# Hop propagation by one-hot matmuls: the order of the blocks in a hop, of the matmuls in a block and of the row fetches

## The chip, the cores and the metric

The kernel runs on one core of one Trainium2 chip. The metric is the device time of one execution in microseconds (us); before the change it is 4582.58 us, the median of three runs (4579.6 to 4584.72). The profile and its trace are of one further execution of 4621.35 us. Engines are named as in the profile: PE (TensorE; PEld are its weight loads), DVE (VectorE), ACT (ScalarE), POOL (GpSimd) and SP (SyncE, which only issues DMAs here).

## The reference

A graph has 10,000 nodes with 128 features and 160,000 edges. Seven times each node takes the weighted sum of the features of its edges' source nodes; the eight versions of every node (the input and seven hops) are then the tokens of a small attention block, which is not touched by the change.

```python
N, deg, D = 10000, 16, 128          # E = N * deg
h = x; toks = [x]
for _ in range(7):
    msg = h[src] * deg_inv_sqrt[src, None] * deg_inv_sqrt[dst, None]
    h = segment_sum(msg, dst, N)
    toks.append(h)
tok = stack(toks, axis=1)
# layernorm, self-attention over the 8 tokens, residual, readout -> (N, D)
```

## The kernel before, in words

**Blocks.** The nodes lie in `NT = 79` blocks of 128. A hop computes the new features of one block after the other from a table of all nodes' features, which is kept twice: in SBUF (`tab[i]`, a 16-bit value and a 16-bit rest, so 256 columns per node) and in HBM (`tabd[i]`). Hops alternate between two tables: hop `k` reads table `k % 2` and writes the other one.

**Edges of a block** are sorted by the block of their source. Sources in blocks 0 to 71 are read from SBUF by PE: `gather(jj)` (L469 to L479) multiplies one-hot 32-wide weight tiles with `tab[:, s, :]`, eight matmuls of 32 columns into one PSUM tile `p`; nine such groups make 72 matmuls. ACT or DVE copies each `p` to an SBUF tile `eb` (L478). `scat` (L441 to L448) then multiplies 128x128 one-hot weights with `eb` and sums into the PSUM tile `acc`: 18 matmuls per block. Sources in blocks 72 to 78 cannot be in that scheme; the block's edges from them (`og0`), and those few that found no free slot (`og1`, the overflow, from any node), are fetched row by row out of HBM by indirect DMAs that POOL issues (L434), and each takes one more 128-wide matmul into `acc`: `fetched` (L454) and the one with weights `Sov` (L464). So a block has 92 matmuls.

**Closing a block.** `over` (L458 to L467) does the `Sov` matmul, DVE sums the two halves of `acc` into `s` (L466), and `fin` (L591 to L598) writes the block's part of the next table: ACT (L593) and DVE (L594) into SBUF, DVE the block's largest value into `mx` (L596), a DMA on ACT's queue the rows to HBM (L597). `token_out` (L492) scales `s` into `r` on POOL (L494) and stores it from SP (L496).

**Order.** `pend` holds work that is put off: two groups of `scat` and the closing of block n-1 are done in block n, behind its gathers. So PE alternates between a gather phase and a scatter phase. The framework schedules the instructions of each engine at build time from the code's order; an engine then runs its own list strictly in order. A fetch waits for all DMA writes of the HBM table that it reads; `og` has two buffers for each of `og0` and `og1`, and SP loads the weights `w` of a block (592 KB, L602) up to four blocks ahead (five buffers).

**Hop 1** (L497 to L551) runs together with the making of the weights (`place`, `matrices`: DVE work above all), on the first table. **Between hop 1 and hop 2**, once the scale is known, ACT and DVE (L148, L149) make the new table in eight chunks, and SP writes each to HBM (L152). **Hops 2 to 7** (L576 to L606) start with a new scale from `mx`, the maximum over all blocks: a transpose on PE (L121), a reduction and four one-element steps on DVE (L123, L137 to L140), a matmul that spreads the value over the partitions (L129), and `c1` (L589), which `fin` needs. The last hop makes no new table and no scale.

**What the names are**: `tb`, `tbs`, `H`, `U`, `dsl` are small tiles of `place`, copied from PSUM by ACT (L329 to L365); `rb` is the row that `matrices` compares with the partition number, loaded by SP (L411); `gsd` are the weights in HBM.

Of the kernel before, what the change touches and what calls it, by code (L numbers as in the profile page):

```python
# [7 lines left out]
F32 = mybir.dt.float32  # L8
# [29 lines left out]
class Hops:  # L38
    def __init__(self, ctx, dp, missing, tc, x, src, dst, dis):
# [5 lines left out]
        self.tabd = [dp.tile([NT * 128, 256], F16, name=f"tabd{i}") for i in range(2)]  # L45
        self.tok = [None] + [dp.tile([NR, D], F32, name=f"tok{k}") for k in range(1, K + 1)]
# [70 lines left out]
    def colmax(self, pp, sp, col):  # L117

        nc = self.nc
        pm = pp.tile([128, 512], F32, name="pm", tag="acc")[0:1, 0:128]  # L120
        nc.tensor.transpose(pm, col, self.ident)  # L121
# [4 lines left out]
    def spread(self, pp, m, out):  # L126
        nc = self.nc
        pb = pp.tile([128, 512], F32, name="pb", tag="acc")[:, 0:1]
# [3 lines left out]
    def pow2(self, pp, sp, col, cap):  # L132

        V = self.nc.vector
        m = self.colmax(pp, sp, col)
# [6 lines left out]
        self.spread(pp, r, q[:, 0:1])  # L142
# [173 lines left out]
    def place(self, ts, got):  # L316
# [49 lines left out]
        V.tensor_scalar(self.oidx[:, a:b, :NI], msc[:, 16:16 + n * NI].rearrange("p (g i) -> p g i", i=NI), float(NG * 512 - 1), None, op0=ALU.add)  # L366
# [61 lines left out]
    def block(self, t, w, tab, tabd, pend, lag, runs, first, evac, fin, drain=True):  # L428

        nc, V, A, T, G = self.nc, self.nc.vector, self.nc.scalar, self.nc.tensor, self.nc.gpsimd  # L430
        og = []
        for i in range(NI + 1):
            o = self.ogp.tile([128, 256], F16, name=f"og{i}")
            G.indirect_dma_start(out=o, out_offset=None, in_=tabd,  # L434
                                 in_offset=bass.IndirectOffsetOnAxis(ap=self.oidx[:, t, i:i + 1], axis=0))
            og.append(o)
        m = 257 if first else 256
        acc = []


        def scat(e, jj):  # L441
            if not acc:
                acc.append(self.pacc.tile([128, 512], F32, name="acc", tag="acc"))
            for j in range(e.shape[1]):
                J = 2 * jj + j
                T.matmul(acc[0][:, :m], w[:, J * 128:(J + 1) * 128], e[:, j, :m], start=J == 0, stop=False)  # L446
                if J == 0 and t > 0:
                    fetched()  # L448


        def fetched():
            for i in range(NI):
                W = w[:, (NG + i) * 128:(NG + i + 1) * 128]
                T.matmul(acc[0][:, :256], W, og[i], start=False, stop=False)  # L454
                if first:
# [625 lines left out]
```

## Time and profile before

| what | value |
|---|---|
| median of 3 runs | 4582.58 us (4579.6 to 4584.72) |
| profiled execution | 4621.35 us |
| its span, first to last instruction | 4619.6 us |
| PE busy | 3902.3 us (84%), 69456 matmuls |
| DVE, ACT, POOL busy | 3437.1, 2441.3, 1853.7 us |
| granted PE clock, mean | 0.961 |
| DMA | 591.53 MB, 128 GB/s |

The profiled execution is 38.8 us (0.8%) longer than the median of the runs. In its span hop 1 lies from about 570 to 1343 us, hops 2 to 7 from there to 3865 us, at some 417 us each, and the attention from about 3870 us to the end. In the lines below a row of the timeline has its start in us from the span's start, its length in us, the engine, the line of the code and the tiles (out<-in); `[0.52 <-X]` is the idle time of that engine just before it and what ended it. An `x72` counts the instructions that are drawn together. Some matmul records are missing from a trace.

### The profile page before, as it was taken

What the parts mean: (1) busy time and instruction counts of PE and PEld (TensorE: products, weight loads), DVE (VectorE), ACT (ScalarE), POOL (GpSimd) and SP (SyncE); (2) the same over time, 40 slices, a digit from 0 to 9 for tenths busy, and PEclk for the clock granted to TensorE, in tenths of its full rate; (3) what the DMA queues carried; (4) which work ended last, traced back from release to release, by engine and by line L of the source; (5) the groups of instructions that cost most, each with busy time, mean ns of one, the idle gap of its engine ahead of it and who ended that gap; (6) DMA issues with size and microseconds to landing.
All of it is one profiled execution on the core that took longest, in us unless ns stands there. A gap on an engine that the chain in (4) does not pass through costs nothing. (4 is left out here: it accounts for less than half of the span.)

```text
span 4619.6 us, 162387 instructions
## 1 busy us (share of the span) xinstructions
PE 3902.3 (84%) x69456; PEld 3011.4 (65%) x69456; DVE 3437.1 (74%) x7291; ACT 2441.3 (53%) x5817; POOL 1853.7 (40%) x1977
## 2 busy tenths in 40 slices
PE   0566389999979999999999899999989997999996
PEld 0566366666656676767676667666767775777775
DVE  6888899999966666666666666666665555999998
ACT  3000045555565555555555555555555555777773
POOL 0000046656644454544444444444544443222221
PEclk9877689999989999999999999999999999999998
DMA  3000044444455555555555555555554554222220
GB/s 112 1 1 1 6 142 149 147 148 147 148 170 172 168 169 161 172 170 167 162 171 170 159 169 168 169 160 170 172 161 155 156 156 114 68 68 74 65 73 11
DMA packets 313745, 591.53 MB, mean 128 GB/s; under 512 B 55032, under 2 KB 206678, under 8 KB 307766
## 3 DMA queue, kind: packets, MB, share of 16 engines
q1 hardware_dynamic: 217925, 476.45, 32.8%
q0 software_dynamic: 35392, 72.55, 5.5%
q10 hardware_dynamic: 59696, 32.08, 2.5%
q8 instruction: 544, 8.91, 0.8%
q14 instruction: 188, 1.53, 0.1%
HBM read 455.43 MB, written 125.46 MB: 126 GB/s over the span
## 5 line engine op out<-in xcount | busy, mean ns | idle before, releaser
L478 ACT CAST eb<-p 128x512 f16<-128x512 f32 x3081 | 1637.7, 595 | 947.4 <-PE p L475 919.5
L434 POOL DMA_INDIRECT og<-tabd,oidx x1106 | 1219.7, 1103 | 2005.5 <-PE acc L454 1016.5
L478 DVE CAST eb<-p 128x512 f16<-128x512 f32 x1896 | 1181.6, 684 | 732.6 <-PE p L475 722.0
L475 PE MATMUL p<-tab,w 128*32 128x256 f16 x39816 | 1495.1, 275 | 208.7 <-DVE eb L478 92.9
L475 PEld LDWEIGHTS <-w 128*32 128x32 fp8e4 x39816 | 977.0, 96 | 645.6 <-issue 602.9
L446 PE MATMUL acc<-eb,w 128*128 128x256 f16 (+1 forms) x9954 | 1349.8, 275 | 9.5 <-DVE indeg L517 8.1
L446 PEld LDWEIGHTS <-w 128*128 128x128 fp8e4 x9954 | 916.3, 98 | 269.6 <-issue 165.0
L494 POOL TENSOR_SCALAR r<-s,ctok 128x128 f32<-128x128 f32 x553 | 452.8, 819 | 152.7 <-DVE indeg L517 67.4
L593 ACT ACTIVATE tab<-s,c 128x128 f16<-128x128 f32 x395 | 158.6, 401 | 296.2 <-DVE s L466 282.7
L594 DVE SCALAR_TENSOR_TENSOR tab<-s,c,tab 128x128 f16<-128x128 f32 x395 | 138.9, 352 | 182.4 <-ACT tab L593 181.9
L466 DVE TENSOR_REDUCE s<-acc 128x128 f32<-128x256 f32 x553 | 229.8, 416 | 38.7 <-PE acc L464 38.2
L823 ACT ACTIVATE junk<-x 128x128 f32<-128x128 f32 x625 | 242.8, 396 | 0.0
L421 DVE TENSOR_TENSOR w<-dsl,iof 128x2432 fp8e4<-128x2432 f16 x79 | 212.2, 2686 | 0.0
L798 PE MATMUL pv<-Wv,xT 128*128 128x131 f32 x1250 | 173.7, 282 | 45.6 <-ACT xT L778 45.6
L881 POOL TENSOR_TENSOR p<-e,in 128x512 f32<-128x512 f32 (+1 forms) x40 | 40.8, 1020 | 419.0 <-DVE e L879 419.0
L262 ACT ACTIVATE U<-U 128x158 f16<-128x158 f32 x25 | 7.6, 302 | 378.1 <-PE U L255 378.1
L275 PE MATMUL ta<-o,ro 128*128 128x158 f16 x1250 | 124.8, 274 | 88.5 <-DVE ro L270 88.5
L798 PEld LDWEIGHTS pv<-Wv,xT 128*128 128x128 f32 x1250 | 151.6, 190 | 61.6 <-ACT xT L778 53.4
L809 PEld LDWEIGHTS po<-v,pT 128*128 128x128 f32 x1250 | 159.5, 194 | 43.3 <-issue 26.5
L275 PEld LDWEIGHTS <-ro 128*128 128x128 f16 x1250 | 119.8, 117 | 92.3 <-DVE ro L270 91.9
L809 PE MATMUL po<-v,pT 128*128 128x128 f32 x1250 | 167.3, 277 | 6.1 <-DVE o L815 6.1
L454 PE MATMUL acc<-og,w 128*128 128x256 f16 x553 | 151.9, 275 | 16.5 <-DMA og<-tabd,oidx 10.8
(260 smaller groups left out, 4350.8 us busy)
## 6 DMA issues: line engine op xcount, KB each, us to landing
w<-gsd SPq DMA_DIRECT2D x474, 592.0 KB
gsd<-w SPq DMA_DIRECT2D x79, 592.0 KB
rb<-srow SPq DMA_DIRECT2D x79, 576.0 KB
tok<-r SPq DMA_DIRECT2D x546, 64.0 KB
x<-tok SPq DMA_DIRECT2D x266, 128.0 KB
tabd<-tab ACTq DMA_DIRECT2D x395, 64.0 KB
og<-tabd,oidx POOLq DMA_INDIRECT x1106
out<-f SPq DMA_DIRECT2D x78, 64.0 KB
```

The costliest lines, as they stand in the source:

```text
L275: T.matmul(ta, ro[:, j, :, i], o12[:, j, :, i], start=j + i == 0, stop=j + i == NP)
L421: V.tensor_tensor(w[:, :NJ * 128].rearrange("p (j d) -> p j d", d=128), dsl[:, g, :, None].to_broadcast([128, NJ, 128]), self.iof1[:, None ...
L434: G.indirect_dma_start(out=o, out_offset=None, in_=tabd, in_offset=bass.IndirectOffsetOnAxis(ap=self.oidx[:, t, i:i + 1], axis=0))
L446: T.matmul(acc[0][:, :m], w[:, J * 128:(J + 1) * 128], e[:, j, :m], start=J == 0, stop=False)
L466: V.tensor_reduce(s, acc[0][:, 0:256].rearrange("p (h d) -> p d h", h=2), axis=X, op=ALU.add)
L475: T.matmul(p[32 * q:32 * q + 32, j], w[:, NJ * 128 + s * CAP:NJ * 128 + (s + 1) * CAP], tab[:, s, :], start=True, stop=True)
L478: (A.copy if evac(jj) else V.tensor_copy)(e[:, :n, 0:256], p[:, :n].rearrange("p j h d -> p j (h d)"))
L494: self.nc.gpsimd.tensor_scalar(r, s, ct[:, t:t + 1], None, op0=ALU.mult)
L593: A.activation(new[:, t, 0:128], s, AF.Copy, scale=c1[:, t:t + 1])
L798: T.matmul(p[:, g - a, :], S[i]["xT"][:, g, :], Wv, start=True, stop=True)
L809: T.matmul(p[:, g - a, :], PT[i % 2][:, g, :], S[i]["v"][:, g, :128], start=True, stop=True)
L823: A.activation(j, S[i]["x"][:, g, :], AF.Square, bias=S[i]["x"][:, g, 0:1], scale=-1.0, accum_out=S[i]["sq"][:, g:g + 1])
```

## The change

**A second, small HBM table.** `tabh` holds blocks 72 to 78 alone. `rows` writes their rows twice, to `tabd` and to `tabh`. `og0` is fetched from `tabh`, the overflow `og1` still from `tabd`; the indices of `og0` count from block 72 on now.

**Order of the blocks.** Hops 2 to 7 go through blocks 72 to 78 first and then through 0 to 71, so `tabh` of the next hop is complete long before a hop ends.

**Fetched tiles first.** In hops 2 to 7 a block's sum in `acc` starts with the matmuls of `og0` and `og1` (`begin`), put right behind its gathers and ahead of the `scat` groups that are left of the block before; the last `scat` matmul ends the sum. The number of matmuls is the same. The first two blocks of a hop (`late`) do their overflow matmul at the end of the sum as before.

**Fetches two blocks ahead.** `ahead(n)` stands behind `begin` of block n and asks for the rows of block n+2. The first two blocks' `og0` are asked for ahead of the hop, their overflow rows (`ogl`) at its first block.

**The scale** is made beside the hop's first block: `scale(0)` behind its gathers, `scale(1)` behind its scatter groups, in PSUM tiles of the gathers' pool.

**Hop 1** keeps its order; its `r` is made by ACT (L519 of the changed code) instead of POOL.

```diff
+        self.tabh = [dp.tile([(NT - 4 * NG) * 128, 256], F16, name=f"tabh{i}") for i in range(2)]
...
     def rows(self, i, tab, t0, t1, eng):
         eng.dma_start(self.tabd[i][t0 * 128:t1 * 128, :].rearrange("(t p) w -> p t w", p=128), tab[:, t0:t1, :])
+        a = max(t0, 4 * NG)
+        if a < t1:
+            o = self.tabh[i][(a - 4 * NG) * 128:(t1 - 4 * NG) * 128, :]
+            eng.dma_start(o.rearrange("(t p) w -> p t w", p=128), tab[:, a:t1, :])
...
-        V.tensor_scalar(self.oidx[:, a:b, :NI], msc[:, 16:16 + n * NI].rearrange("p (g i) -> p g i", i=NI), float(NG * 512 - 1), None, op0=ALU.add)
+        V.tensor_scalar(self.oidx[:, a:b, :NI], msc[:, 16:16 + n * NI].rearrange("p (g i) -> p g i", i=NI), -1.0, 0.0, op0=ALU.add, op1=ALU.max)
...
-    def block(self, t, w, tab, tabd, pend, lag, runs, first, evac, fin, drain=True):
+    def fetch(self, t, i, src, name=None):
+
+        o = self.ogp.tile([128, 256], F16, name=name or f"og{i}", bufs=2 if name else None)
+        self.nc.gpsimd.indirect_dma_start(out=o, out_offset=None, in_=src[0] if i == NI else src[1],
+                                          in_offset=bass.IndirectOffsetOnAxis(ap=self.oidx[:, t, i:i + 1], axis=0))
+        return o
+
+    def block(self, t, w, tab, og, pend, lag, runs, first, evac, fin, lead=False, late=False, mid=None, ahead=None):
...
+        def fetched(i, start=False, stop=False):
+            W = w[:, (NG + i) * 128:(NG + i + 1) * 128] if i < NI else self.Sov[:, t, :]
+            T.matmul(acc[0][:, :256], W, og[i], start=start, stop=stop)
...
+        def begin():
+            acc.append(self.pacc.tile([128, 512], F32, name="acc", tag="acc"))
+            for i in range(NI if late else NI + 1):
+                fetched(i, start=i == 0)
...
-                T.matmul(acc[0][:, :m], w[:, J * 128:(J + 1) * 128], e[:, j, :m], start=J == 0, stop=False)
-                if J == 0 and t > 0:
-                    fetched()
+                T.matmul(acc[0][:, :m], w[:, J * 128:(J + 1) * 128], e[:, j, :m], start=first and J == 0,
+                         stop=J == NG - 1 and not (first or late))
...
+            if first or late:
+                T.matmul(acc[0][:, :256], self.Sov[:, t, :], og[NI], start=False, stop=True)
             s = self.fp.tile([128, 128], F32, name="s")
...
             for _ in range(n):
                 gather(jj)
                 jj += 1
-            while drain and len(pend) > lag:
+            if mid:
+                mid(0)
+            if not first:
+                begin()
+                ahead()
+            while len(pend) > lag:
                 pend.pop(0)()
+            if mid:
+                mid(1)
...
-        self.nc.gpsimd.tensor_scalar(r, s, ct[:, t:t + 1], None, op0=ALU.mult)
+        if k == 1:
+            self.nc.scalar.activation(r, s, AF.Copy, scale=ct[:, t:t + 1])
+        else:
+            self.nc.gpsimd.tensor_scalar(r, s, ct[:, t:t + 1], None, op0=ALU.mult)
...
-                if not last:
-                    mc = self.sp.tile([128, 1], F32, name="mc")
-                    V.tensor_reduce(mc, mx, axis=X, op=ALU.max)
-                    V.tensor_mul(mc, mc, self.rho)
-                    q = self.pow2(self.pacc, self.sp, mc, 2.0 ** 8)
-                    V.tensor_mul(self.sinv, self.sinv, q[:, 1:2])
-                    V.tensor_scalar(c1, self.dis2, q[:, 0:1], None, op0=ALU.mult)
+                def scale(part, c1=c1, mx=mx):
+                    if part == 0:
+                        mc = self.sp.tile([128, 1], F32, name="mc")
+                        V.tensor_reduce(mc, mx, axis=X, op=ALU.max)
+                        V.tensor_mul(mc, mc, self.rho)
+                        scale.m = self.colmax(self.pg, self.sp, mc, "p")
+                    else:
+                        q = self.pow2_of(self.pg, self.sp, scale.m, 2.0 ** 8, "p")
+                        V.tensor_mul(self.sinv, self.sinv, q[:, 1:2])
+                        V.tensor_scalar(c1, self.dis2, q[:, 0:1], None, op0=ALU.mult)
...
-                        nc.scalar.dma_start(dout[t * 128:(t + 1) * 128, :], new[:, t, :])
+                        self.rows(i, new, t, t + 1, nc.scalar)
...
-                for t in range(NT):
+                order = [*range(4 * NG, NT), *range(4 * NG)]
+                og = [[None] * (NI + 1) for _ in order]
+                def ahead(n, og=og, order=order, din=din):
+                    if n + 2 < NT:
+                        for j in range(NI):
+                            og[n + 2][j] = self.fetch(order[n + 2], j, din)
+                    for m in range(0 if n == 0 else n + 2, min(n + 3, NT) if n >= 0 else 0):
+                        og[m][NI] = self.fetch(order[m], NI, din, "ogl" if m < 2 else None)
+
+                ahead(-2)
+                ahead(-1)
+                for n, t in enumerate(order):
```

**What stands where, 1: PE at the start of hop 3** (every later hop reads the same). Before, the first block's last scatter matmul there, then its two fetched tiles and the next block's first; `og` are fetched tiles, `eb` gathered ones, `Sov` and `w` weights:

```order
L446 MATMUL acc<-eb_245,w 128x256
L454 LDWEIGHTS w
L454 MATMUL acc<-og_31152,w 128x256
L464 LDWEIGHTS Sov
L464 MATMUL acc<-og_31154,Sov 128x256
L446 LDWEIGHTS w
L446 MATMUL acc<-eb_247,w 128x256
L454 LDWEIGHTS w
L454 MATMUL acc<-og_31263,w 128x256
```

Now, from the last gather matmul of the first block to the transpose of the scale:

```order
L492 MATMUL p<-tab_231,w 32x256
L454 LDWEIGHTS w
L454 MATMUL acc<-og_31142,w 128x256
L468 LDWEIGHTS w
L468 MATMUL acc<-eb_21104,w 128x256
...
L468 MATMUL acc<-eb_21110,w 128x256
L123 MATMUL pm<-ident,mc 1x128
```

The fetched tile opens the block's sum, the scale's transpose moved from the midst of the second block's gathers to behind eight scatter matmuls, and the overflow matmul went behind the second block's gathers. On DVE two more copies of gathered tiles stand between the maximum (L616) and the step ahead of that transpose (L617), where one stood before.

**2: POOL at the same place.** Before, behind the last block's `r`, six fetches of the new hop's table, in pairs of `og0` and `og1`:

```order
L494 TENSOR_SCALAR r<-s,ctok_233 128x128 x3
L434 DMA og_31152<-tabd_143,oidx 128x256
L434 DMA og_31154<-tabd_143,oidx 128x256
L434 DMA og_31263<-tabd_143,oidx 128x256
L434 DMA og_31265<-tabd_143,oidx 128x256
L434 DMA og_31390<-tabd_143,oidx 128x256
L434 DMA og_31392<-tabd_143,oidx 128x256
L494 TENSOR_SCALAR r<-s,ctok_234 128x128
```

Now:

```order
L439 DMA og_31142<-tabh_145,oidx 128x256
L521 TENSOR_SCALAR r<-s,ctok_235 128x128
L439 DMA og_31144<-tabh_145,oidx 128x256
L521 TENSOR_SCALAR r<-s,ctok_235 128x128 x2
L439 DMA og_31247<-tabh_145,oidx 128x256
L439 DMA ogl<-tabd_143,oidx 128x256 x2
L439 DMA og_31253<-tabd_143,oidx 128x256
```

The first two blocks' `og0` moved ahead of the last blocks' `r`, and the first fetch that needs the whole table is that of the first two blocks' overflow.

**3: POOL at the start of hop 2**, where the table was only just made. Before:

```order
L574 MEMSET tab_229 128x512
L434 DMA og_21178<-tabd_144,oidx 128x256
L434 DMA og_21180<-tabd_144,oidx 128x256
L434 DMA og_21289<-tabd_144,oidx 128x256
L434 DMA og_21291<-tabd_144,oidx 128x256
```

Now:

```order
L602 MEMSET tab_231 128x512
L439 DMA ogl<-tabd_144,oidx 128x256 x2
L439 DMA og_21272<-tabd_144,oidx 128x256
L439 DMA og_21161<-tabh_146,oidx 128x256
L439 DMA og_21163<-tabh_146,oidx 128x256
```

The first block's `og0` (`og_21161`) was the first of the list and is now the fourth, behind three overflow fetches. In the same place SP writes `tabh` behind the last chunk of `tabd` and ahead of the weights of the hop's third block, which stood ahead of `tabd` before; and PE's list holds two blocks' gathers and the first five matmuls of the third ahead of that `og0`, where it held all gathers of three blocks and the first scatter groups.

More of the change, by code (lines that the diff above doesn't have):

```diff
@@ L124, in colmax, with spread @@
         return m
-    def spread(self, pp, m, out):
+    def spread(self, pp, m, out, tag="acc"):
         nc = self.nc
-        pb = pp.tile([128, 512], F32, name="pb", tag="acc")[:, 0:1]
+        pb = pp.tile([128, 512], F32, name="pb", tag=tag)[:, 0:1]
         nc.tensor.matmul(pb, self.ones32, m, start=True, stop=True)
@@ L526, in hop1 @@
                 for t, w in zip(quads[q], W[q]):
-                    yield from self.block(t, w, self.tab[0], self.tabd[0], pend, 2, (2, 2, 2, 3), True, lambda jj: True, fin1)
+                    og = [self.fetch(t, j, (self.tabd[0], self.tabh[0])) for j in range(NI + 1)]
+                    yield from self.block(t, w, self.tab[0], og, pend, 2, (2, 2, 2, 3), True, lambda jj: True, fin1, t == 0)
             for _ in self.place(quads[0], dsl[0]):
@@ L578, in run @@
                 tab, new = self.tab[i], self.tab[1 - i]
-                din, dout = self.tabd[1 - i], self.tabd[i]
+                din = self.tabd[1 - i], self.tabh[1 - i]
                 ct, c1, mx, mo = self.ctok[i], self.c1[i], self.mx[i], self.mx[1 - i]
```

44 lines of the change are left out of this document (19 added, 25 removed).

## The prediction

> **What bounds the kernel now.** I read the page for the span, the stretches by stage, the timeline of a block in the midst of a hop and of the place where one hop follows another, and the groups of hop 1. The page's span, and the stretches of hop 1 and of one later hop (length, then busy us and instructions of PE, PEld, DVE, ACT, POOL, then clock and DMA):
>
> ```profile
> span 4619.6 us, 162387 instructions
> ```
> ```profile
> 570.00:1300.00 730.00, 658.72 (x11700) 490.06 (x11698) 705.72 (x1035) 407.56 (x855) 430.15 (x219) 0.97 0.46 147
> 2620.00:3030.00 410.00, 377.26 (x7158) 284.50 (x7161) 261.41 (x546) 235.38 (x466) 202.84 (x236) 1.00 0.54 168
> ```
>
> Hop 1 is DVE's (705.72 of 730 us), a later hop PE's (377.26 of 410). A block in the midst of a hop:
>
> ```profile
> 2402.21 0.41 DVE L466 TENSOR_REDUCE s<-acc 128x128 f32<-128x256 f32 x1
> ...
> 2403.39 1.38 PE L475 MATMUL p<-tab,w 128*32 128x256 f16 x43
> ...
> 2404.23 0.58 ACT L478 CAST eb<-p 128x512 f16<-128x512 f32 x1 [1.17 <-PE p L475]
> ...
> 2405.01 2.48 DVE L478 CAST eb<-p 128x512 f16<-128x512 f32 x4 [1.38 <-PE p L475]
> ...
> 2406.31 0.61 PE L446 MATMUL acc<-eb,w 128*128 128x256 f16 x4
> ...
> 2406.98 0.27 PE L454 MATMUL acc<-og,w 128*128 128x256 f16 x1
> ...
> 2407.42 0.41 DVE L466 TENSOR_REDUCE s<-acc 128x128 f32<-128x256 f32 x1
> ```
>
> A block takes 2407.42 - 2402.21 = 5.21 us: a gather phase of 2406.31 - 2403.39 = 2.92, then the scatter phase, whose matmuls follow each other at (2406.98 - 2406.31) / 6 = 0.11 us. PE waits for no fetch here. The starts of hops 3 to 7 are otherwise. Stretches of 26 us from the last closing (L466) of hops 2 to 6, with PE alone, and one from the midst of a hop:
>
> ```profile
> 1779.26:1805.26 26.00, 21.18 (x365) 0.93 0.44 126
> 2195.80:2221.80 26.00, 21.62 (x394) 0.93 0.46 135
> 2611.17:2637.17 26.00, 19.29 (x358) 0.93 0.41 121
> 3028.80:3054.80 26.00, 20.24 (x354) 0.87 0.40 120
> 3446.02:3472.02 26.00, 19.66 (x355) 0.80 0.39 116
> 2800.00:2826.00 26.00, 24.22 (x468) 1.00 0.54 166
> ```
>
> 468 matmuls in 26 us are 18.0 per us. The five starts fall short by 103, 74, 110, 114 and 113, together 514, or **28.6 us**. The timeline of the fourth shows where:
>
> ```profile
> 3028.62 2.07 PEld L475 LDWEIGHTS <-w 128*32 128x32 fp8e4 x73 [0.21 <-issue]
> 3028.62 2.27 PE L475 MATMUL p<-tab,w 128*32 128x256 f16 x72
> 3028.80 0.42 DVE L466 TENSOR_REDUCE s<-acc 128x128 f32<-128x256 f32 x1 [0.58 <-PE acc L464]
> ...
> 3030.38 0.33 ACTq L597 DMA_DIRECT2D tabd<-tab  x1
> ...
> 3031.06 0.22 DVE L585 TENSOR_REDUCE mc<-mx 128x1 f32<-128x79 f32 x1
> ...
> 3032.00 0.27 PE L121 MATMUL pm<-ident,mc 128*1 128x128 f32 x1 [0.41 <-DVE mc L586]
> ...
> 3034.56 0.38 PE L129 MATMUL pb<-r,ones 1*128 1x1 f32 x2 [0.42 <-DVE r L140]
> ...
> 3035.24 1.01 POOL L434 DMA_INDIRECT og<-tabd,oidx  x1 [5.32 <-PE pb L129]
> ...
> 3037.96 0.27 PE L454 MATMUL acc<-og,w 128*128 128x256 f16 x1 [0.52 <-DMA og<-tabd,oidx]
> ...
> 3039.47 0.27 PE L464 MATMUL acc<-og,Sov 128*128 128x256 f16 x1 [1.25 <-DMA og<-tabd,oidx]
> ...
> 3042.32 0.37 PE L454 MATMUL acc<-og,w 128*128 128x256 f16 x1 [2.47 <-issue]
> ...
> 3042.49 2.98 PE L446 MATMUL acc<-eb,w 128*128 128x256 f16 x13
> ...
> 3045.40 3.49 PE L475 MATMUL p<-tab,w 128*32 128x256 f16 x72
> ...
> 3055.09 0.41 DVE L466 TENSOR_REDUCE s<-acc 128x128 f32<-128x256 f32 x1
> ```
>
> The new hop's gathers start at once. The first fetch waits until the last table rows, issued at 3030.38, have landed: 3035.24. (The page puts it to L129, which has nothing to do with it.) From there PE waits for fetch after fetch, 0.52, 1.25 and 2.47 us, and then runs slowly: 72 gathers in 3.49 us where they took 2.27.
>
> **The change part by part.**
>
> *The midst of a hop, 5.21 us a block: 0.* The same 92 matmuls. The closing now starts after six matmuls of the phase instead of five, 0.11 us later; DVE's idle 1.38 us before its next copies covers that. A second DMA of ACT in seven blocks of each hop costs 0.33 (as L597 does), inside ACT's idle 1.17; without that cover 35 x 0.33 = 11.6 us in five hops. The fetches have two blocks, 10.4 us, where issue to use took 3037.96 - 3035.24 = 2.7.
>
> *The start of hops 3 to 7: -25 us.* The fourth start again, with the new order. Gathers of the first block until 3028.62 + 2.27 = 3030.89. Its `og0` lies there, asked for a block ago. That matmul and eight scatter matmuls take to 3030.89 + 0.21 (PEld's gap at a change of phase) + 9 x 0.11 = 3032.1. The scale's transpose waits for DVE: in the old order it started at 3032.00 with one copy behind L585; one more (2.48 / 4 = 0.62) gives 3032.62, so **0.5 us idle**. The spreading matmul came 3034.56 - 3032.00 = 2.56 later with two copies between; those are gone, 1.3 us, at 3033.9. PE's ten other matmuls last as long. Second block's gathers from about 3034.6 to 3037.5, then the overflow matmul, which now is the first to need the landed table: its fetch is issued at 3035.24 as the first one was, and used at 3037.96. So the new wait, under 0.3 us, stands in for 4.2. First closing at 3038.3, the third two blocks on at 3048.7, instead of 3055.09: 6.4 us, against 6.3 by count (114 / 18.0). Five starts by count: 28.6, less 0.7 us each that is still waited: 25. Ends: 20 (1.5 us more each, if the overflow fetch comes as late as the second one did, 3039.47) and 30.
>
> How much of that is clock? Granted clock in the starts' rows is 0.80 to 0.93. In the fourth the slow stretch cost 3.49 - 2.27 = 1.2, and 2.98 - 13 x 0.11 = 1.5: 2.7 us of the 6.3. [...]
>
> *The start of hop 2: +6 us.*
>
> ```profile
> 1366.36 2.15 PE L475 MATMUL p<-tab,w 128*32 128x256 f16 x72
> ...
> 1372.70 1.00 POOL L434 DMA_INDIRECT og<-tabd,oidx  x1 [11.72 <-DMA w<-gsd]
> ...
> 1374.01 0.95 POOL L434 DMA_INDIRECT og<-tabd,oidx  x1 [0.30 <-issue]
> ...
> 1375.38 0.37 PE L454 MATMUL acc<-og,w 128*128 128x256 f16 x1 [0.61 <-DMA og<-tabd,oidx]
> ...
> 1379.98 3.25 PE L446 MATMUL acc<-eb,w 128*128 128x256 f16 x17
> ```
>
> Here the whole table has to land first (1372.70), `tabh` last of all. The first `og0` is now POOL's fourth fetch: 1372.70 + 3 x 1.31 + 2.7 = 1379.3, and PE's list stops there. Before, PE had by 1379.98 done the third block's 72 gathers, 13 more, and the first block's 20 scatter matmuls and two fetched ones: 107, at 18.0 per us 5.9 us. Ends: +4 (one load of weights less lies ahead of the table) and +9 (the extra `tabh` write ahead of the third block's weights, and the clock).
>
> *Hop 1: -1 us.* POOL's `r`, ACT's nearest operation, ACT's wait ahead of `tbs`, a DVE operation that runs beside `r`, and DVE's wait for `rb` (us, times, longest):
>
> ```profile
> L494 POOL TENSOR_SCALAR r<-s,ctok x79: 602/2412/5055, 606.4 to 1343.5; 128x128 f32<-128x128 f32 x79
> ```
> ```profile
> L518 ACT ACTIVATE tab<-s,dis 128x128 f32<-128x128 f32 x78 | 31.5, 404 | 42.7 <-DVE s L466 41.7
> L348 ACT CAST tbs<-tb 76x128 f16<-76x128 f32 x39 | 10.2, 261 | 72.1 <-PE tb L347 71.4
> ```
> ```profile
> L421 DVE TENSOR_TENSOR w<-dsl,iof x79: 2673/2684/2848, 574.4 to 1318.2; 128x2432 fp8e4<-128x2432 f16 x79
> ```
> ```profile
> DVE w L418 <- DMA rb<-srow: 6.2, 6, 2.3
> ```
>
> ACT gets 79 x 0.404 = 32 us more of its 407.56 in 730. It often comes just ahead of `tbs`, where ACT idled 72.1 / 39 = 1.85 us for PE; that covers it. DVE's list is the same. SP no longer holds its queue for an `r` of 2.4 us (median), so the rows `rb` come a little earlier. Ends: -6 (all of DVE's wait for `rb`) and +3 (a tenth of the 32 shows); 32 if nothing covers is a rival. I take -1, nearer to no change, since SP's queue is only a part of what `rb` waits for.
>
> *Rest: 0.* The attention and the table of the first hop have the same lists but for one small write.
>
> Sum: -25 + 6 - 1 = **-20 us**: 4621.35 to 4601 in a profiled execution, and by the same difference 4582.58 to **4562.6 us** in the runs.
>
> **The rivals.**
>
> *A. The clock falls all the same (0.11).* If the wait for the overflow and the scale are enough idle to halve the clock at each start, 2.7 us x 5 = 13.5 of the 25 stay: -25 + 13.5 + 6 - 1 = -6.5, 4576. For it: even the start that loses least (394 matmuls) shows 0.93. Against it: the waits that I find sum to under 1 us per start. That is no change within what can be told (0.2%, 9 us).
>
> *B. Slower: ACT's `r` in hop 1 lies on DVE's path (0.09).* DVE has 24 us of idle in those 730, so what delays it is paid in full. `r` has one buffer, and waits on ACT for its last store; behind it stand the copies of `tbs` and `dsl` that DVE's next steps read. Uncovered, 32 us: 4582.58 - 19 + 32 = 4596. It decides from 19 / 32, 60% of each `r`, on. Against it: the 1.85 us above.
>
> *C. The overflow fetch is late (0.05)*: the lower end above, 4568, still faster.
>
> *D. Hop 1 gains much (0.03).* If POOL's `r` held up DVE as DVE holds up `r` (2412 ns against 602), up to 79 x 0.602 = 48 us would go: 4516. [...] In the trace only POOL pays: L421 takes 2673 to 2848 ns, 2684 in the median, with `r` beside it or not.
>
> **How the numbers follow.** Forecast 0.72, A 0.11, B 0.09, C 0.05, D 0.03. Faster by over 0.2%: 0.72 + 0.05 + 0.03 = 0.80; same: A, 0.11; slower: B, 0.09. The forecast's own range, from -30 + 4 - 3 to -20 + 9 + 1 (not all ends at once in hop 1), is 4554 to 4573; with A it reaches 4577, and B, D and a little at the lower end stay out, so 4553 to 4577.
>
> **What would show it.** Right: 26 us from a hop's last closing hold 440 matmuls or more with clock 1.00, the first `og0` of hops 3 to 7 is on POOL ahead of the last closing, hop 2's first closing comes some 6 us later, a block still takes 5.2 us, hop 1 ends where it did. Wrong: a block of 5.25 us or more (0.04 x 474 eats the gain), waits of PE for `og` or `ogl` of over 1 us per start, DVE idle ahead of L366 or L397 in hop 1, or ACT waiting for the store of `r`.

## The result, and the profile after

The changed kernel takes **4445.84 us**, the median of four runs (4444.40 to 4450.52), and the kernel before 4583.65 in four runs beside it (4579.60 to 4585.35). The ratio is **0.970, with a 95% interval of 0.969 to 0.972**: 138 us faster. I had forecast 4562.6 and a range of 4553 to 4577. (Of all runs below one, of the version "amid the gathers", showed a lower granted clock, 0.867, took 4477.80 us and is left out.)

The page's span of the changed kernel, and its stretches of hop 1 and of one later hop, as for the kernel before:

```profile
span 4442.6 us, 162333 instructions
```
```profile
570.00:1300.00 730.00, 659.85 (x11791) 489.44 (x11788) 707.44 (x1042) 427.85 (x936) 259.47 (x149) 0.98 0.46 147
2620.00:3030.00 410.00, 397.12 (x7689) 304.03 (x7688) 282.71 (x597) 245.44 (x500) 215.93 (x252) 1.00 0.57 181
```

Hop 1 is much as it was. In the later hop PE does 7689 matmuls where it did 7158. The closings that part the stages, by the timelines of before (L466) and of after (L483): the last of hop 1, the first of hop 2, the last of hop 7.

```profile
1342.74 0.42 DVE L466 TENSOR_REDUCE s<-acc 128x128 f32<-128x256 f32 x1 [3.37 <-PE acc L464]
1377.34 0.42 DVE L466 TENSOR_REDUCE s<-acc 128x128 f32<-128x256 f32 x1 [8.94 <-PE acc L464]
3864.95 0.42 DVE L466 TENSOR_REDUCE s<-acc 128x128 f32<-128x256 f32 x1 [1.53 <-PE acc L464]
```
```profile
1336.37 0.42 DVE L483 TENSOR_REDUCE s<-acc 128x128 f32<-128x256 f32 x1 [3.54 <-PE acc L481]
1376.84 0.42 DVE L483 TENSOR_REDUCE s<-acc 128x128 f32<-128x256 f32 x1 [1.54 <-PE acc L481]
3688.98 0.43 DVE L483 TENSOR_REDUCE s<-acc 128x128 f32<-128x256 f32 x1 [1.19 <-PE acc L468]
```

Hop 1 ends 6.4 us earlier, the start of hop 2 takes 40.47 us instead of 34.60, **hops 2 to 7 take 2312.1 instead of 2487.6**, and the rest is alike. The spans differ by 177 us, the runs by 138: the profiled execution of before was 38.8 us longer than its runs, that of after was not. A block in the midst of a hop, in the timeline of the changed kernel:

```profile
2401.26 0.94 POOL L439 DMA_INDIRECT og<-tabd,oidx  x1 [0.31 <-issue]
...
2401.67 2.62 PE L492 MATMUL p<-tab,w 128*32 128x256 f16 x72
...
2402.24 0.62 POOL L521 TENSOR_SCALAR r<-s,ctok 128x128 f32<-128x128 f32 x1
...
2402.76 2.54 ACT L495 CAST eb<-p 128x512 f16<-128x512 f32 x5 [1.49 <-PE p L492]
2402.86 2.48 DVE L495 CAST eb<-p 128x512 f16<-128x512 f32 x4 [1.01 <-PE p L492]
2404.22 0.28 PE L454 MATMUL acc<-og,w 128*128 128x256 f16 x1
2404.34 0.27 PE L454 MATMUL acc<-og,Sov 128*128 128x256 f16 x1
2404.45 2.13 PE L468 MATMUL acc<-eb,w 128*128 128x256 f16 x18
2404.78 1.01 POOL L439 DMA_INDIRECT og<-tabh,oidx  x1 [1.92 <-PE acc L454]
...
2406.51 0.73 PE L492 MATMUL p<-tab,w 128*32 128x256 f16 x20
```

In the block of before that is shown in the prediction, POOL's two fetches and its `r` lay so:

```profile
2402.10 1.01 POOL L434 DMA_INDIRECT og<-tabd,oidx  x1 [2.28 <-PE acc L454]
...
2403.41 0.94 POOL L434 DMA_INDIRECT og<-tabd,oidx  x1 [0.30 <-issue]
...
2404.39 0.62 POOL L494 TENSOR_SCALAR r<-s,ctok 128x128 f32<-128x128 f32 x1
```

The block takes 2406.51 - 2401.67 = **4.84 us instead of 5.2**. The scatter phase is as long as before (2.29); the gather phase fell from 2.92 to 2.55. Before, DVE's first copy came 1.62 us after the first gather (2405.01 - 2403.39), now 1.19 (2402.86 - 2401.67); ACT and DVE then copy without a gap. Both wait for PE to report a finished `p` tile (`<-PE p`), though PE has long issued the matmuls of the first tiles. (A report is a raise of the semaphore for which ACT and DVE wait.) The trace holds the moments at which PE's semaphore is raised. Counted from the first gather, with POOL's second fetch of the block beside them:

```
kernel   second fetch    PE's reports (us after the first gather)
before    0.02 to 0.96    0.82  1.60  1.69  1.79  1.88  1.97  2.19 ...
after    -0.41 to 0.53    1.07  1.16  1.25  1.34  1.44  1.61  2.15 ...
```

PE starts a tile's eight gathers every 0.22 us at first. Yet in before one report gets through beside the fetch and the next only 0.64 us behind its end, in after the first comes 0.54 us behind its end; then five come 0.09 us apart, which can't be the pace of tiles that take PE 0.22 us each. They look held up. So two theories for the 0.36 us. **SIGNALS**: while POOL issues an indirect fetch, PE's reports come late; what decides is where the second fetch falls against the gather phase. The first fetch of a block waits for the matmul that lets its buffer go (`<-PE acc L454`), and the second follows 0.3 us behind it. The change moved that matmul from inside the scatter phase to its head, so that both come 0.43 us earlier against the gathers. **PORT**: DVE's first copy starts within 0.1 us of the end of POOL's `r` in 430 of the 474 blocks of before and 439 of after (within 0.05 us in 366 and 388); `r` keeps it out. Two more stood beside them: **ORDER** (the matmuls' order is itself quicker) and **ROWS AHEAD** (the earlier asking pays).

### The profile page after: what moved, and what is told of

Its sections match the earlier page's. It is cut to its first block, busy times and chain, and to the rows that moved or that the text cites. A ratio compares the mean times of both kernels' runs of the same rounds, so it can differ in the third digit from the quotient of the medians.

```text
span 4442.6 us, 162333 instructions
## 1 busy us (share of the span) xinstructions
PE 3840.0 (86%) x69456; PEld 3004.5 (68%) x69456; DVE 3436.7 (77%) x7291; ACT 2421.8 (55%) x5896; POOL 1672.6 (38%) x1898
## 5 line engine op out<-in xcount | busy, mean ns | idle before, releaser
L495 ACT CAST eb<-p 128x512 f16<-128x512 f32 x3081 | 1597.9, 602 | 936.4 <-PE p L492 886.0
L492 PE MATMUL p<-tab,w 128*32 128x256 f16 x39816 | 1437.5, 275 | 110.1 <-ACT eb L495 35.9
L468 PE MATMUL acc<-eb,w 128*128 128x256 f16 (+1 forms) x9954 | 1244.3, 274 | 16.1 <-DVE indeg L544 8.0
L439 POOL DMA_INDIRECT og<-tabh,oidx x553 | 626.5, 1133 | 1632.4 <-PE acc L454 871.0
L468 PEld LDWEIGHTS <-w 128*128 128x128 fp8e4 x9954 | 954.0, 98 | 175.9 <-issue 61.8
L439 POOL DMA_INDIRECT og<-tabd,oidx x541 | 557.0, 1030 | 458.6 <-PE acc L481 276.6
L521 POOL TENSOR_SCALAR r<-s,ctok 128x128 f32<-128x128 f32 x474 | 296.6, 626 | 39.6 <-DVE s L483 25.6
L483 DVE TENSOR_REDUCE s<-acc 128x128 f32<-128x256 f32 x553 | 228.6, 413 | 25.2 <-PE acc L481 18.5
```

The source lines that it names most:

```text
L439: self.nc.gpsimd.indirect_dma_start(out=o, out_offset=None, in_=src[0] if i == NI else src[1], in_offset=bass.IndirectOffsetOnAxis(ap=self ...
L483: V.tensor_reduce(s, acc[0][:, 0:256].rearrange("p (h d) -> p d h", h=2), axis=X, op=ALU.add)
L492: T.matmul(p[32 * q:32 * q + 32, j], w[:, NJ * 128 + s * CAP:NJ * 128 + (s + 1) * CAP], tab[:, s, :], start=True, stop=True)
L495: (A.copy if evac(jj) else V.tensor_copy)(e[:, :n, 0:256], p[:, :n].rearrange("p j h d -> p j (h d)"))
L521: self.nc.gpsimd.tensor_scalar(r, s, ct[:, t:t + 1], None, op0=ALU.mult)
```

## The experiments

**Four kernels on one chip, and a surprise.** The edits, in turn: before with `r` of hops 2 to 7 on ACT; after with the fetched matmuls back in their old places; after with them amid the gathers; after without most fetches.

```diff
+        if k > 1:
+            self.nc.scalar.activation(r, s, AF.Copy, scale=ct[:, t:t + 1])
+        else:
             self.nc.gpsimd.tensor_scalar(r, s, ct[:, t:t + 1], None, op0=ALU.mult)
```


> The kernel before, with POOL's multiplication r of hops 2 to 7 put on ACT and nothing else. Theory SIGNALS (while POOL issues an indirect fetch, PE's reports of finished p tiles reach ACT and DVE late, so the block is set by where the second fetch falls in the gather phase): the fetches stay where they are, DVE's first copy still starts about 1.6 us after the first gather, the block stays 5.2 us, the time within 0.5% of the kernel before (4560 to 4605). Theory PORT (r on POOL keeps DVE's first copy waiting until r ends): DVE's first copy starts 0.7 to 1.1 us after the first gather, the block falls to 4.8 to 4.9 us, the time to about 4583 - 474 x 0.35 = 4415. Theory ORDER (the place of the fetched matmuls in the scatter phase is itself what costs): 5.2 us, no change.

```diff
-                if first and J == 0 and not lead:
+                if J == 0 and not lead:
                     for i in range(NI):
                         fetched(i)
...
-            if first or late:
+            if True:
                 T.matmul(acc[0][:, :256], self.Sov[:, t, :], og[NI], start=False, stop=True)
...
-                begin()
                 ahead()
```


> The changed kernel with one part undone: the fetched matmuls stand again behind J = 0 and the overflow matmul at the closing; rows are still asked for two blocks ahead, the blocks keep the new order and the scale its new place. SIGNALS: the buffers of the fetched rows come free 0.4 to 0.7 us later, the second fetch starts at the first gather again instead of 0.4 us ahead of it, and the block goes back to 5.1 to 5.2 us: 4446 + 474 x 0.36 = 4615, or, by what the unprofiled runs of the kernel before show, from 4570. A rival, ROWS AHEAD (the gain comes from rows that are asked for earlier): the block stays 4.83, the time 4440 to 4455. ORDER: 5.2 us, as SIGNALS; PORT: 5.2 us too, since r stands behind the second fetch.

```diff
                 gather(jj)
                 jj += 1
+                if not first and jj == 5:
+                    begin()
+                    ahead()
```


> The changed kernel with the two fetched matmuls of a block, and the fetches behind them, put behind the fifth of the nine gathers of p instead of behind the ninth. SIGNALS: the first fetch starts some 1.6 us after the first gather and the second ends some 2.3 us later, 3.9 us, so that the next gather phase is free of them but for 0.2 us: the first copies start 0.5 to 0.8 us after the first gather, a block takes 4.4 to 4.5 us, the time 4446 - 474 x 0.38 = 4265 (4240 to 4310). PORT: r, behind the second fetch, ends about as late against the next gather phase as in the changed kernel, or later: 4.8 us, 4446 within 1%. ORDER: fetched matmuls amid the gathers change PE between two kinds of work twice more, 4.83 or up to 5.2, 4446 to 4600.

```diff
-                    if n + 2 < NT:
+                    if n + 2 < 2:
...
+                    elif n + 2 < NT:
+                        for j in range(NI):
+                            og[n + 2][j] = og[n % 2][j]
...
+                        og[m][NI] = self.fetch(order[m], NI, din, "ogl") if m < 2 else og[m % 2][NI]
```


> The changed kernel with the fetches of hops 2 to 7 left out but for the first two blocks of each hop, whose rows the other blocks use again: so the rows that spill over a cell are the wrong ones from the third block on. Every matmul, copy and r stays. SIGNALS: nothing holds up PE's reports, the block takes what 92 matmuls take, 4.35 to 4.4 us, and the time is about 4446 - 474 x 0.46 = 4228, less 1 to 3 us for each start of a hop: 4205 to 4235. ORDER: the order of the matmuls is the changed kernel's, 4.83 us, 4440 to 4450. PORT: r ends before the gather phase's first copies, as SIGNALS for the block.

On this chip the kernel before takes **4260.56 us** (13 runs), not 4584. The first edit takes 4259.20 (ratio 0.9997, 0.9988 to 1.0007), old places 4214.43 (0.989, 0.987 to 0.991), amid the gathers 4308.52 (1.011, 1.009 to 1.013), without fetches 4211.24 (0.988, 0.987 to 0.990). Blocks take 4.37 us with `r` on ACT, with old places and without fetches: here a fetch costs nothing. Amid the gathers they take 4.59: PE changes twice more between kinds of matmul there, which I take for the 0.22 more, though no run shows it alone. That its time lies in the range given for SIGNALS is chance, since nothing is held up on this chip. The first edit's block on this chip (call it B):

```profile
2400.75 0.94 POOL L434 DMA_INDIRECT og<-tabd,oidx  x1 [0.30 <-issue]
...
2400.80 2.15 PE L475 MATMUL p<-tab,w 128*32 128x256 f16 x72
2401.25 2.54 ACT L478 CAST eb<-p 128x512 f16<-128x512 f32 x5 [0.60 <-PE p L475]
2401.47 2.48 DVE L478 CAST eb<-p 128x512 f16<-128x512 f32 x4 [0.53 <-PE p L475]
```

The same fetch lies at the start of the gathers, but DVE copies 0.67 us after the first gather. So in hops 2 to 7 the chips differ in this, and the theories have to be told apart on one like the first. **The changed kernel once more, and hop 1's `r` alone:**

> The changed kernel, as it is, beside the kernel before on the same chip. In the four runs before this one the kernel before took 4261 us where it had taken 4583, with blocks of 4.37 us instead of 5.2: PE's reports came every 0.22 us there, fetch or no fetch. SIGNALS says that where the kernel before takes 4260 the changed one gains nothing in the midst of a hop (4.37 in both), and comes out by hop 1 and the starts of the hops alone, 4205 to 4240; and where the kernel before takes 4580, 4446 again, with blocks of 4.83. ORDER: the gain of 3% is there on any chip, 4130 where before takes 4260.

```diff
-        if k == 1:
+        if k == 0:
             self.nc.scalar.activation(r, s, AF.Copy, scale=ct[:, t:t + 1])
```

> The changed kernel with r of hop 1 on POOL again, as before. By my forecast's term for hop 1 (-1, ends -6 and +3) the time is that of the changed kernel plus 1 us. Against it: in a run above, r on POOL in hop 1 and nothing else of the change there, hop 1's last closing came at 1362, in the runs with r on ACT at 1323 to 1329; rival D (POOL's r holds up DVE in hop 1) then says 30 to 35 us more than the changed kernel where reports are not held up, and 7 us more where they are.

Another chip, and 4591.68 (before), 4451.67 (after, ratio 0.970, 0.967 to 0.972) and 4453.04 (`r` of hop 1 on POOL): the result comes again, and `r` of hop 1 is worth 1.4 us, too little to tell from none. On the chips of all later runs before took 4585 to 4588. **Four kernels there.** The edit of the fourth:

```diff
+            if gate and jj == 0:
+                gate(e)
...
-            self.ogp = c.enter_context(tc.tile_pool(name="og2", bufs=2))
+            self.ogp = c.enter_context(tc.tile_pool(name="og2", bufs=3))
...
+                def gate(n, e, order=order):
+                    if n + 2 < NT:
+                        ix[0] = self.fp.tile([128, NI + 1], I32, name="ix")
+                        V.scalar_tensor_tensor(ix[0], e[:, 0, 0:NI + 1], 0.0, self.oidx[:, order[n + 2], :], op0=ALU.mult, op1=ALU.add)
```


> The changed kernel again, beside the kernel before and the three below on the same chip. SIGNALS (while POOL issues an indirect fetch, PE's reports of finished tiles come late; on some chips, as the first experiments showed, not on all): if the kernel before takes about 4590 here, this one takes 4450 with blocks of 4.83 us; if before takes 4260, PE's reports come every 0.22 us, the block is 4.37 in both kernels and this one takes 4205 to 4240.

> The changed kernel with the fetched matmuls behind J = 0 and the overflow matmul at the closing again. Where before takes 4590: SIGNALS has the second fetch start at the first gather again, a block of 5.1 to 5.2 us, and 4450 + 474 x 0.33 = 4606 (4570 to 4620); ROWS AHEAD (it is the earlier asking that pays) keeps 4.83 and 4450. Where before takes 4260: 4.37 and 4214, as measured.

> The changed kernel without the fetches of hops 2 to 7 but those for the first two blocks of each hop (the others use these rows again, so rows that spill over are the wrong ones). Where before takes 4590: SIGNALS has the reports every 0.22 us, 4.37 us a block and 4450 - 473 x 0.46 = 4232, less 1 to 4 us for each start, so 4210 to 4235, the time that it took on the other chip; ORDER has 4.83 and 4450. Where before takes 4260: 4211, as measured.

> The changed kernel with its two fetches per block moved in time and nothing else: DVE makes the block's two columns of row numbers again behind its first copy of the block (and out of the first tile that ACT copied, so that it can't come earlier), the fetches read these, and the fetched rows have three buffers each, so that no matmul lets them go. The first fetch then starts some 1.7 us after the first gather, the second ends some 2.3 us later, 4.0, and r follows. SIGNALS: the first copies start 0.5 to 0.9 us after the first gather, the block is 4.37 to 4.5 us on either kind of chip; where before takes 4590 that is 4450 - 473 x 0.40 = 4260 (4230 to 4310), where before takes 4260 it is 4205 to 4240. ORDER: the matmuls are where they are in the changed kernel, so 4.83 us. PORT: r now ends as late against the next gather phase as in the changed kernel, 4.7 to 4.9 us.

Measured, beside 4587.87 for before: after 4450.22 (0.970, 0.968 to 0.971), **old places 4580.97 (0.999, 0.998 to 1.000)**, **without fetches 4227.41 (0.922, 0.920 to 0.923)**, **gate 4310.68 (0.939, 0.938 to 0.941)**; blocks of 4.84, 5.12, 4.37 and 4.50 us. The timelines of the last three:

```profile
2404.47 2.07 PE L492 MATMUL p<-tab,w 128*32 128x256 f16 x56
2404.49 0.95 POOL L439 DMA_INDIRECT og<-tabh,oidx  x1 [0.31 <-issue]
...
2405.98 2.48 DVE L495 CAST eb<-p 128x512 f16<-128x512 f32 x4 [1.26 <-PE p L492]
```
```profile
2402.50 2.15 PE L492 MATMUL p<-tab,w 128*32 128x256 f16 x72
2402.95 2.54 ACT L495 CAST eb<-p 128x512 f16<-128x512 f32 x5 [0.90 <-PE p L492]
2403.17 2.48 DVE L495 CAST eb<-p 128x512 f16<-128x512 f32 x4 [0.54 <-PE p L492]
```
```profile
2401.55 0.95 POOL L439 DMA_INDIRECT og<-tabd,ix  x1 [0.31 <-issue]
...
2402.39 2.27 PE L492 MATMUL p<-tab,w 128*32 128x256 f16 x72
...
2403.22 0.69 DVE L495 CAST eb<-p 128x512 f16<-128x512 f32 x1 [0.58 <-PE p L492]
```

DVE's first copy comes 1.51, 0.67 and 0.83 us after the first gather, with the second fetch at 0.02, none, and from -0.84 to 0.11. Old places and no fetches came out as SIGNALS had it, the gate 0.7 us above its range. In the gate, PE's list is the changed kernel's; what differs is the fetches' time (with a third buffer and one small DVE step), and the block is 0.34 us shorter. On chip B, where nothing is held up, old places and the changed order without fetches both take 4.37: ORDER is out. ROWS AHEAD is out as the cause of the gain: old places keep the earlier asking and lose 131 of the 138 us. **PORT, and a version meant to be better:**

> The kernel before with r of hops 2 to 7 on ACT and nothing else, meant for a chip on which the kernel before takes about 4590. PORT (r on POOL keeps DVE's first copy waiting until r ends: in the trace of before that copy starts within 0.05 us of r's end in nine blocks of ten): the block falls from 5.2 to 4.8 or 4.9 us, the time to about 4590 - 474 x 0.35 = 4425. SIGNALS: r only happens to end when the reports held up by the second fetch come through; the fetches stay, the block stays within 0.15 us of 5.2 and the time within 1.5% of before (4520 to 4600). Where before takes 4260: no difference, as measured.

```diff
+            if gate and jj == 0:
+                gate(p)
...
+                    x = ix[0] if n >= 0 else None
+                    if n + 2 < NT:
+                        og[n + 2][0] = self.fetch(order[n + 2], 0, din, None, x)
+                    if n >= 0:
+                        og[n][NI] = self.fetch(order[n], NI, din, None, x)
```


> A version built on SIGNALS. The changed kernel with the fetches put where nothing waits for PE's reports: in each block DVE makes the row numbers again ahead of its first copy (out of the first p tile, so not earlier than that), POOL then issues og0 for the block after next and og1 for this block, and the overflow matmul stands at the closing in every block, so that the five fetches in a row at the start of a hop are one per block too. SIGNALS: the first fetch starts some 1.3 us after the first gather and the second ends at 3.6 us; a block takes 4.37 to 4.45 us, the first closing of hops 3 to 6 comes 10 to 11 us after the last one instead of 14.4: where before takes 4590, 4450 - 473 x 0.42 - 4 x 4 = 4235 (4205 to 4275). Where before takes 4260: 4200 to 4230. ORDER: 4.83 us a block, 4450 or more.

`r` on ACT: **4586.17 beside 4587.37, ratio 0.9997 (0.9986 to 1.0007)**. PORT falls. Its block, with no `r` on POOL:

```profile
2400.82 0.95 POOL L434 DMA_INDIRECT og<-tabd,oidx  x1 [0.30 <-issue]
...
2400.86 2.12 PE L475 MATMUL p<-tab,w 128*32 128x256 f16 x56
...
2401.66 0.58 ACT L478 CAST eb<-p 128x512 f16<-128x512 f32 x1 [0.84 <-PE p L475]
2402.41 1.89 DVE L478 CAST eb<-p 128x512 f16<-128x512 f32 x3 [1.30 <-PE p L475]
```

DVE's copy still comes 1.55 us after the first gather. This and the block on chip B are one program at one place:

```
chip              second fetch     PE's reports (us after the first gather)
this one          -0.05 to 0.90    0.78  1.53  1.62  1.71  1.80  1.91  2.13 ...
B                 -0.05 to 0.89    0.43  0.65  0.87  1.09  1.30  1.52  1.74 ...
```

On B a report comes every 0.22 us, on this one only the first gets through while the fetch lasts, the second 0.75 us later, and the four after that follow 0.09 to 0.11 us apart. The one block is typical. In 440 of the 474 blocks of before three reports or more come in such a burst, and in the middle eight tenths of them it starts 0.57 to 0.64 us behind the end of a fetch; 0.50 to 0.57 in after (441 blocks), 0.51 to 0.56 in old places (440), 0.59 to 0.64 with `r` on ACT (440) and with the gate (415). So in these runs the burst follows the fetch wherever that lies, and the hold outlasts POOL's own time by those 0.50 to 0.64 us. Without fetches, and on chip B with `r` on ACT, no block has such a burst among its gathers. It also explains PORT's look: `r`, 0.6 us long, starts at the fetch's end as well.

My better version took 4648.80 (1.013, 1.011 to 1.015), with blocks of 5.20, far from the 4205 to 4275 that I had worked out from SIGNALS. Its timeline shows what I had left out:

```profile
2403.80 1.49 PE L492 MATMUL p<-tab,w 128*32 128x256 f16 x48
...
2405.03 2.00 DVE L497 CAST eb<-p 128x512 f16<-128x512 f32 x3
2405.25 2.54 ACT L497 CAST eb<-p 128x512 f16<-128x512 f32 x5 [0.79 <-DVE ix L656]
2405.39 1.01 POOL L439 DMA_INDIRECT og<-tabh,ix  x1 [0.66 <-DVE ix L656]
...
2406.70 0.95 POOL L439 DMA_INDIRECT og<-tabd,ix  x1 [0.30 <-issue]
...
2407.27 0.27 PE L481 MATMUL acc<-og,Sov 128*128 128x256 f16 x1
...
2408.20 0.69 DVE L497 CAST eb<-p 128x512 f16<-128x512 f32 x1 [1.17 <-PE acc L481]
2408.80 0.41 DVE L483 TENSOR_REDUCE s<-acc 128x128 f32<-128x256 f32 x1
```

Now the report of the last tile is held, until 0.53 us behind the second fetch's end: DVE's fourth copy waits 1.17 us and the closing queues behind it. The next block's row numbers (`ix`) stand behind the closing on DVE, and its first copies behind them. The next two runs put this to the test (first the gate behind ACT's first copy, then also overflow rows one block earlier; each edit is shown against the version before it):

```diff
-                gate(p)
+                gate(e)
```

> The version of the last call with one thing altered: DVE makes the row numbers behind its first copy of a block, out of the first tile that ACT copied, as in the version that took 4311, and not ahead of it. The first fetch then starts about 1.9 us after the first gather instead of 1.2, the second ends at about 4.2. SIGNALS: the reports of the middle tiles and of the closing come through ahead of or between the fetches, DVE's fourth copy no longer comes 1.2 us behind its third, the block is 4.45 to 4.55 us instead of 5.2, and with one overflow fetch per block the first closing of hops 3 to 6 comes 10 to 11.5 us after the last one instead of 14.5: where before takes 4590, 4311 - 4 x 3.5 = 4297 (4265 to 4320). If the slow block of the last version has another cause than the place of the fetches (the closing's overflow matmul in every block, or the two added columns): 5.1 to 5.2 us and 4600 to 4650. Where before takes 4260: 4200 to 4240.

> The changed kernel again, for the comparison on the same chip: 4450 with blocks of 4.84 us where before takes 4590; where before takes 4260, 4205 to 4240 with blocks of 4.37, the gain being hop 1 and the starts of the hops (ORDER: 4130).

```diff
-                    if n >= 0:
-                        og[n][NI] = self.fetch(order[n], NI, din, None, x)
+                    for m in range(max(n, 0) + (n > 2), min(n + 1 + (n > 1), NT)):
+                        og[m][NI] = self.fetch(order[m], NI, din, None, x, 1 if m > n else 2)
```


> The version that took 4424, with the overflow row asked for one block earlier (blocks 0 to 2 of a hop as there, block 2 asks for its own and the next one's). In the trace of the version that took 4424 PE waited 122.7 us in 130 blocks for rows of that fetch, asked for some 4 us ahead, and 15.2 us more with no cause shown. If late rows are all that its blocks of 5 to 6 us come from, nearly all take 4.50 us and the time is 4424 - 138 = 4286 (4270 to 4310). If the waits are the reports' (SIGNALS at another place), the irregular blocks stay and the time with them, 4400 to 4430. Where before takes 4260: 4200 to 4240.

The first took 4424.43 (0.964, 0.962 to 0.967; after on the same chip 4449.21), more than I expected: its blocks take 4.50 us, but many 5 to 6. PE's waits name the cause:

```profile
PE acc L481 <- DMA og<-tabd,ix: 122.7, 130, 4.3
```

Asked for some 4 us ahead, the rows came late: 122.7 us in 130 waits. Asked for a block earlier they cost 7.7 us in 5 waits: nearly all blocks take 4.50 us, and the time is 4333.97 (0.945, 0.943 to 0.947). That is more than the 4286 of the sum: one or two blocks in a hop take some 8 us, and in hops 2 to 6 the third-last takes 7.2 to 7.9, where the next hop's first fetches fall amid the gathers. The others were not traced to a cause. The **best version is the plain gate, 4310.68**, 6% under before.

## Why the prediction was wrong, point by point

**"The midst of a hop, 5.21 us a block: 0": the step that failed.** It measured -0.36 us a block in the profiles, and about 131 us in the runs by the undoing (4580.97 against 4450.22). In the profiles the terms came to -167 us (midst), -8.7, +5.9 and -6.4, against 0, -25, +6 and -1. I counted matmuls and the closing's 0.11 us, and took DVE's idle 1.38 us ahead of its copies for cover. It was the bound: that idle, with `<-PE p` beside it, said that DVE waited for tiles whose matmuls had been issued, and 72 gathers that took 2.27 us at a hop's start and 2.92 in its midst said the same. I used the first as a cushion and never asked about the second. What I also left out: a matmul that moves takes along the fetch that waits for its buffer. None of my four rivals held this, and the only sign of "wrong" that I gave for a block was a longer one.

**"The start of hops 3 to 7: -25".** From a hop's last closing to the third of the next it took 25.06, 24.07, 25.79, 26.29 and 25.83 us before, and takes 24.51, 23.75, 24.14, 23.70 and 22.20 now, where I had 19.9: **-8.7 in all**. The 26 us from the last closings hold 403, 389, 391, 401 and 437 matmuls, not 440. Four of the five first closings come 14.2 to 14.6 us after the last one, not 9.5. The start of hop 5 shows the wait that I missed:

```profile
2533.21 2.37 PE L492 MATMUL p<-tab,w 128*32 128x256 f16 x63
...
2533.91 0.94 POOL L439 DMA_INDIRECT ogl<-tabd,oidx  x1 [2.72 <-DMA tabd<-tab]
...
2535.16 0.95 POOL L439 DMA_INDIRECT ogl<-tabd,oidx  x1 [0.31 <-issue]
...
2536.41 0.94 POOL L439 DMA_INDIRECT og<-tabd,oidx  x1 [0.30 <-issue]
...
2536.72 0.58 ACT L495 CAST eb<-p 128x512 f16<-128x512 f32 x1 [1.64 <-PE p L492]
...
2537.66 0.94 POOL L439 DMA_INDIRECT og<-tabh,oidx  x1 [0.30 <-issue]
...
2538.91 0.94 POOL L439 DMA_INDIRECT og<-tabd,oidx  x1 [0.30 <-issue]
...
2539.57 0.58 ACT L495 CAST eb<-p 128x512 f16<-128x512 f32 x1 [2.27 <-PE acc L481]
...
2542.23 0.41 DVE L483 TENSOR_REDUCE s<-acc 128x128 f32<-128x256 f32 x1
```

Five fetches stand in a row, and ACT's copies come one in 2.2 to 2.9 us. Without three of them (and the later ones) the first closings of hops 3 to 6 come after 10.4 to 10.6 us and the third after 19.4 to 19.8; with one overflow fetch per block the first come after 9.3 to 11.0. So most of what was missing is the held reports. Not all: the third closing agrees with my 19.9 in part by luck, since the first comes 1 us later than my 9.5 and the blocks behind it are shorter than my 5.2. PE still waits there for the first block's overflow rows, 1.04, 0.37 and 1.44 us in hops 3 to 5, where I had under 0.3.

**"The start of hop 2: +6"**: 40.47 - 34.60 = +5.9, by the mechanism named. PE stops for the first `og0`, POOL's fourth fetch:

```profile
1372.49 0.37 PE L454 MATMUL acc<-og,w 128*128 128x256 f16 x1 [3.02 <-DMA og<-tabh,oidx]
```

That is 36.1 us behind hop 1's end, where I had 36.6 (1379.3 - 1342.7).

**"Hop 1: -1"**: -6.4 in the profile, just past the end of -6. The only part that I moved for, `r` on ACT, is worth 1.4 us, within the scatter of the runs; hop 1 ends anywhere from 1334.7 to 1341.0 us in the runs with the change's other parts, so no more of it can be assigned.

**The rivals.** A, the clock, came in part: in 26 us from the last closings it was granted 0.93 at three starts and 1.00 at two, where it had been 0.80 to 0.93 at all five. My -25 took it that the waits of 0.5 and 0.3 us leave the clock alone; that was my assumption, and no run shows it. Before, the clock was 0.55 in the 6.6 us from 3042.30, behind 5.5 us in which PE was busy for 1.29. After, PE's longest single waits were 0.81 and 1.35 us at the two starts with 1.00, and 1.09, 0.81 and 3.98 us at the three with 0.93. B (ACT's `r`) didn't show. C (late overflow rows) did at the start of hop 7, which makes no scale and so comes to the overflow matmul sooner: PE waited 3.98 us for `ogl`, used 4.0 us after it was asked for, where I had 2.7. In the version at 4424 rows asked for some 4 us ahead were late too. D (POOL's `r` holds up DVE in hop 1) didn't show: with hop 1's `r` back on POOL the time rose by only 1.4 us (4451.67 to 4453.04). D's look-alike in hops 2 to 7, PORT, had nine blocks of ten for it and was nothing: taking `r` off POOL moved the time by 1.2 us of 4587.

## What to carry to other kernels

When an engine waits for a tile whose matmuls were issued long ago, ask what holds up the report, before you count that idle as cover. When a matmul is moved, move in thought the DMA that waits for its buffer, and see what it will run beside. And undo one part alone on the same chip: a copy that started at the end of another engine's operation in nine blocks of ten shared a cause with it, and did not wait for it.

## What the hardware showed that I had not expected

- In the runs of before, after, old places, the gate and `r` on ACT (4586.17), PE's semaphore raises come late beside an indirect fetch of POOL and for 0.50 to 0.64 us behind its end: 0.75 to 0.78 us from one to the next in the blocks shown of before and of `r` on ACT, then a burst 0.09 to 0.11 us apart. Without the fetches, with POOL's `r` still there, they come 0.22 us apart. What in the fetch holds them was not found.
- One chip showed none of it: 4260.56 us where the others take about 4587 for the same kernel, 7%. The changed kernel itself was not run on it; old places (4214.43) and no fetches (4211.24) take nearly the same there, so its place of the matmuls should bring little on that chip. Hop 1 also ended 33 to 39 us earlier there with the change's parts than in before with `r` of hops 2 to 7 moved (1362.0). With hop 1's `r` on POOL, DVE waits 28.7 us there for `rb`, with `r` on ACT 5.2 to 6.3 (on the first chip 6.2 and 2.8), and L421 takes 2682 ns in the median as ever, so that wait, rather than D, looks to be part of it; why there and not on the others stays open.
